# Normalising tokens on VectorE, storing token blocks later, and loading the first pairs' rows in another sequence

## The chip, the core and the metric

The kernel runs on one core of a Trainium2 chip. The metric is the time of one execution on the device, in microseconds. The core has a matrix engine (TensorE, "PE" in the profile), three engines for element-wise work (VectorE, "DVE"; ScalarE, "ACT"; GpSimd, "POOL"), and an engine that does little but issue transfers (SyncE, "SP"). Each engine takes its instructions in the order in which the program was written for it; an instruction that must wait for another engine or for a transfer holds up those behind it on its own engine.

## What is computed

`x` is 2048 tokens of 512 numbers, fp32.

```python
def _A_ref(x, wqkv, wo):                 # 32 heads of 16, no mask
    qkv = (x @ wqkv) -> q, k, v per head
    p = softmax(q k^T * Dh**-0.5)
    return (p @ v, heads side by side) @ wo

def _B_ref(x, w1, w3, w2):               # F = 1792
    h = silu(x @ w1) * (x @ w3)
    return h @ w2

xn = layernorm(x)                        # (x - mean) / sqrt(var + 1e-5)
s = _A_ref(xn, wqkv, wo)
g = silu(_B_ref(xn, w1, w3, w2))
return x + s * g
```

## The kernel before

**Arithmetic.** A product of two fp32 matrices whose precision matters is done as three matmuls: each side is split into a high part and a low part (`xth` and `xtl`, `wh` and `wl`), and high x high, high x low and low x high are added up in one bank of the accumulator memory. So whatever is to be multiplied has first to be split: one engine copies the rounded high part, another subtracts it from the original.

**Two parts.** A prologue (lines 446 to 657) normalises and transposes the tokens, makes the value rows of all heads and the key and query rows of the first four pairs of heads, and finds the score maxima of the first half pair. It takes about 112 of the 1727 us. The main part then runs, for 16 pairs of heads, the scores, the exponentials and the products with the values, and between them the SwiGLU layer and the key and query rows of later pairs. There the order of TensorE's instructions is written out by hand as a string (`ORDER_OF_ISSUE`), and a small model of costs in the program decides only when the helpers of other engines are issued. In the prologue the order on every engine is simply the order of the Python statements.

**The prologue's path for a token tile** (`t`, 128 tokens; four tiles make a block `b` of 512). `load_x` brings `x` to `xin`. `spread` makes mean and variance on VectorE (`st` L492, `mv` L494, `ve` = variance + eps L496) and `rs` = `ve` to the power -1/2 on POOL (L498). `norm` makes `xn` = (`xin` - mean) * `rs` (L505), for the first two tiles on VectorE and for the others on POOL. `transposed` transposes it in four pieces on TensorE (L514), copies the high part on ACT (`xth`, or `xeh` for even blocks, L517) and subtracts on VectorE (`xtl`, `xel`, L518). The two halves of a block are `xts[b]`; `xt` is the pair of tiles that holds blocks 1 and 3.

**Per block.** `token_rows(b, 1)` makes the block's key rows and `token_rows(b, 0)` its query rows (`sh` and `sl`, high and low, for four pairs of heads at once), and stores them to DRAM (`qk`: `sh` by a transfer that ACT issues, L609; `sl` by one that SP issues, L610). `token_values(b, i)` makes the value rows of tile `i`, and ACT issues their store (`v<-vrow`, L547). `beside(b, n)` does score products (L419) of the first pair, four to six at a time, each followed by a maximum on VectorE (L421).

**Loads back from DRAM.** Key and query rows come back with the pairs' heads on other partitions: `load_k(p, cols)` (L398) and `load_q(p, half, cols)` (L407) issue six transfers each on SP. For pair 0, `ks` is loaded block by block as the blocks are made; `load_k(1)` loads all 2048 columns of pair 1. `load_v(1)` (L390) loads the values of the second group of heads into `vt`, at the end of the prologue. `max_rows` turns the maxima into rows `mh` and `ml`, which four small transfers put into `qs` (L446); the first exponential's score product (L675) reads them.

**Weights.** `Weights` streams the units of the SwiGLU weights and of the later projections: `load` (L325) brings a unit to `wr`, `pump` splits it on POOL (L339, L340), `start` issues the first three loads, `fill` issues more as buffers come free.

**Copies of the token blocks.** `xts` of all blocks do not fit in the core's memory, so each block is copied to DRAM (`xt_d`, L624, two transfers of 1 MB) at the top of the block loop. The main part (`gate`) begins with block 3, which is still in place, and fetches blocks 0, 1 and 2 back in pieces later, and block 3 once more for the last projections.

**Completion semaphores.** Each transfer that SP or ACT issues takes one of eight completion semaphores, in turn over both engines, and its issue waits until the transfer that held that semaphore before has landed. In the built program these are the names DMAHW0 to DMAHW7. So adding or moving a transfer changes which earlier one each later one has to wait for.

Of the kernel before, what the change touches and what calls it, by code (L numbers as in the profile page):

```python
# [12 lines left out]
ALU = mybir.AluOpType  # L13
# [8 lines left out]
KC = D // P  # L22
NT = S // P
TB = 4
# [122 lines left out]
def raw(ap):  # L147
    return ap.bitcast(F32)
# [3 lines left out]
def kernel(ctx: ExitStack, tc: tile.TileContext, x, wqkv, wo, w1, w3, w2, out):  # L152
    nc = tc.nc
# [30 lines left out]
    xt_d = [[dram.tile([P, KC * 512], F32R, name=f"xt{b}{s}") for s in range(2)] for b in range(TB)]  # L184
# [23 lines left out]
    def run(gen):  # L208
        for _ in gen:
            pass  # L210
# [105 lines left out]
    class Weights:  # L316
# [37 lines left out]
        def next(self):  # L354

            i = self.taken
            self.taken += 1
            self.pump()
            return i, self.parts.pop(i)
# [4 lines left out]
    wts = Weights()  # L364

    def room_between(n, hf):

        return {0: (0, 2, 5, FH), 1: ()}[hf] if n < KC - 1 else ()
# [23 lines left out]
    def load_k(p, cols=slice(0, S)):  # L392
        t = ks[p % 2]
        for h in range(2):
            r = (p % 4) * 32 + h * DH
            kh, kl = (raw(v)[r:r + DH, cols] for v in qk_d[4 + p // 4])
            for n, src in enumerate((kh, kl, kh)):
                nc.sync.dma_start(raw(t)[64 * h + n * DH:64 * h + (n + 1) * DH, cols], src)  # L398

    def load_q(p, half, c=None):  # L400
        t = qs[p % 2]
        c = c or slice(half * 1024, (half + 1) * 1024)
        for h in range(2):
            r = (p % 4) * 32 + h * DH
            qh, ql = (raw(v)[r:r + DH, c] for v in qk_d[p // 4])
            for n, src in enumerate((qh, qh, ql)):
                nc.sync.dma_start(raw(t)[64 * h + n * DH:64 * h + (n + 1) * DH, c], src)  # L407
# [41 lines left out]
    with tc.tile_pool(name="pro", bufs=1) as pro, tc.tile_pool(name="pros", bufs=1) as pros:  # L449
        wv = [[pro.tile([P, D], F32R, name=f"wv{v}{k}") for v in "hl"] for k in range(KC)]  # L450
        wqk = [[pro.tile([P, KC, P], F32R, name=f"w{c}{v}") for v in "hl"] for c in "qk"]
        xin = [pro.tile([P, D], F32, tag="xin", name=f"xin{t}", bufs=9) for t in range(4)]

        def load_x(t):
            if t >= 4:
                xin.append(pro.tile([P, D], F32, tag="xin", name=f"xin{t}", bufs=9))
            nc.sync.dma_start(xin[t], x[t * P:(t + 1) * P, :])
# [29 lines left out]
        xts = {}  # L487

        def spread(t):

            st = pro.tile([P, 6], F32, tag="st", name="st", bufs=3)
            nc.vector.bn_stats(st, xin[t])  # L492
            mv = pro.tile([P, 2], F32, tag="mv", name="mv", bufs=3)
            nc.vector.bn_aggr(mv, st)  # L494
            ve = pro.tile([P, 1], F32, tag="ve", name="ve", bufs=3)
            nc.vector.tensor_scalar_add(ve, mv[:, 1:2], EPS)  # L496
            rs = pro.tile([P, 1], F32, tag="rs", name="rs", bufs=3)
            nc.gpsimd.tensor_tensor(rs, ve, minus, op=ALU.pow)  # L498
            return mv, rs

        def norm(t, mv=None, rs=None):
            if mv is None:
                mv, rs = spread(t)
            xn = pro.tile([P, D], F32, tag="xn", name="xn", bufs=5)
            (nc.vector if t < 2 else nc.gpsimd).tensor_scalar(xn, xin[t], mv[:, 0:1], rs, op0=ALU.subtract, op1=ALU.mult)  # L505
            return xn

        def transposed(t, xn):
            b, tt = divmod(t, 4)
            if tt == 0:  # L510
                xts[b] = xt_pair(keep) if b % 2 else even_pair()
            ps = bank("m")
            for k in range(KC):
                nc.tensor.transpose(ps[:, k * P:(k + 1) * P], xn[:, k * P:(k + 1) * P], ident)  # L514
            hi, lo = (v[:, :, tt * P:(tt + 1) * P] for v in xts[b])
            src = ps.rearrange("p (k t) -> p k t", k=KC)
            nc.scalar.copy(hi, src)  # L517
            nc.vector.tensor_sub(lo, src, raw(hi))  # L518
# [32 lines left out]
        xn = {0: norm(0)}  # L551
# [35 lines left out]
        def beside(b, n):  # L587

            for _ in range(groups.get((b, n), 0)):
                max_unit(*next(early))  # L590
            if (b, n) == (TB - 1, 4):
                next(first_rows)
                next(first_rows)
# [3 lines left out]
        def token_rows(b, c):  # L597

            hi, lo = xts[b]
            rbk = KC * c  # L600
            ps = bank("e")
            for k in range(KC):
                run(split3(ps, [w[:, k, :] for w in wqk[c]], (hi[:, k, :], lo[:, k, :]), k == 0, k == KC - 1))
            sh = pros.tile([P, 512], F32R, tag="sh", name="sh", bufs=3)
            sl = pros.tile([P, 512], F32R, tag="sl", name="sl", bufs=3)
            nc.scalar.copy(sh, ps)
            nc.vector.tensor_sub(sl, ps, raw(sh))
            cols = slice(b * 512, (b + 1) * 512)
            nc.scalar.dma_start(raw(qk_d[rbk][0])[:, cols], raw(sh))  # L609
            nc.sync.dma_start(raw(qk_d[rbk][1])[:, cols], raw(sl))  # L610

        def more_tokens(n):

            if n < NT:
                transposed(n, xn.pop(n))
                if n + 4 < NT:
                    load_x(n + 4)
                if n + 2 < NT:
                    xn[n + 2] = norm(n + 2)

        for b in range(TB):
            cols = slice(b * 512, (b + 1) * 512)
            for s in range(2):
                nc.sync.dma_start(raw(xt_d[b][s]), raw(xts[b][s]).rearrange("p k t -> p (k t)"))  # L624
            token_rows(b, 1)
            if b == TB - 1:
                load_k(0, cols)
                wts.start()
            beside(b, 0)
            more_tokens(4 * b + 4)  # L630
            if b == 0:
                nc.gpsimd.memset(*next(blank))
                nc.gpsimd.memset(*next(blank))
                more_tokens(5)
            token_rows(b, 0)
            if b < TB - 1:
                load_k(0, cols)
            else:
                load_k(1)
            beside(b, 1)  # L640
            more_tokens(4 * b + (5 if b else 6))
            if b == 0:
                nc.gpsimd.memset(*next(blank))
                nc.gpsimd.memset(*next(blank))
                more_tokens(7)
                load_q(0, 0, cols)
                continue
            for i in range(TB):
                run(token_values(b, i))
                if i == 0 and b < TB // 2:  # L650
                    load_q(0, 0, cols)
                if i == 0 and b == TB - 1:
                    load_q(0, 1)
                    wts.pump(KC)
                    wts.fill()
                if i == 1 and b == 2:
                    load_q(1, 0)
                beside(b, 2 + i)
                if i < 2:
                    more_tokens(4 * b + 6 + i)  # L660
# [99 lines left out]
    def gate():  # L760

        xt = xts[TB - 1]
# [3 lines left out]
        def fetch_tokens(b):  # L766
            pieces.extend((b, s, k) for s in range(2) for k in range(KC))

        def some_tokens():
            for b, s, k in [pieces.pop(0) for _ in range(min(2, len(pieces)))]:  # L770
                nc.sync.dma_start(raw(rows2[s])[:, k, :], raw(xt_d[b][s])[:, k * 512:(k + 1) * 512])
# [21 lines left out]
        for n, b in enumerate(ORDER):  # L793
# [4 lines left out]
            for hf in range(HF):  # L798
# [49 lines left out]
                def counted():  # L848

                    if since[0] is not None:  # L850
                        since[0] += 1
                        if since[0] == 2:
                            since[0] = None
                            fetch_tokens(rest[0])
                    some_tokens()

                for f in range(FH):
                    if f in room_between(n, hf):
                        for e in rows_here():
                            yield e  # L860
                            number += 1
                    for up in range(2):
                        counted()
                        i, w = wts.next()
                        mms = [m for k in range(KC) for m in three([v[:, k, :] for v in w], [v[:, k, :] for v in xt])]
                        yield lambda j, mms=mms: mms[j], 3 * KC, [i], (lambda ps, i, f=f: upped(ps, i, f)) if up else gated, None
                        if up:
                            ups.append(number)
                        number += 1
# [28 lines left out]
                for t in range(4):  # L898
# [10 lines left out]
                    if t > 1 and hf == 1 and n + 1 < TB:  # L909
                        if t == 2:  # L910
                            xt = xt_pair(keep)
                        nc.sync.dma_start(raw(xt[t - 2]).rearrange("p k t -> p (k t)"), raw(xt_d[ORDER[n + 1]][t - 2]))
                    yield down, 3 * FH, [i for i, _ in ws] if t == 3 else [], (
                        lambda ps, i, t=t: summed(ps, i, t)), ups
# [316 lines left out]
    for g in range(KC - 1):  # L1231
        p = 4 * g + 3
# [204 lines left out]
    for t in range(4):  # L1437
        i, ps = take("o")
# [30 lines left out]
```

## Time and profile before

| | |
|---|---|
| median of 3 runs (lowest, highest) | 1729.66 us (1729.29, 1730.66) |
| the profiled execution's own time | 1728.91 us |
| its span in the profile | 1727.1 us |
| mean granted TensorE clock | 0.994 |
| TensorE busy | 1702.8 us, 99% of the span |
| VectorE busy | 1375.0 us, 80% |
| ACT busy | 1221.4 us, 71% |
| POOL busy | 882.8 us, 51% |

All later rows come from that one execution. A row such as `28.45 0.15 DVE L496 TENSOR_SCALAR ve<-mv 128x1 ...` is a line of the timeline: start and duration in microseconds, engine, line of the program, operation, output from input, and in square brackets how long the engine stood still before it and what ended that. "SPq" and "ACTq" are issues of transfers by SP and ACT, so the duration is that of the issue and not of the transfer. A row that starts with two times and a colon is a stretch of the span: its length, then busy time (and number of instructions) of the engines in the order PE, PEld (weight load), DVE, ACT and POOL, then the granted TensorE clock (1.00 is full speed), and at the end the busy share of the transfer engines and the GB/s they moved.

### The profile page before, as it was taken

How to read it: one execution, taken by the hardware profiler on the slowest of the kernel's cores; microseconds unless marked ns; L12 is line 12 of the kernel's file. 1: busy time of each engine (PE TensorE's matmuls, PEld its weight loads, DVE VectorE, ACT ScalarE, POOL GpSimd, SP SyncE). 2: the span in 40 equal slices, each digit the busy share in tenths (PEclk: the TensorE clock that was granted, in tenths of full speed). 3: DMA queues.
4: the chain of work that ended last, by engine and by line, in shares of the span. 5: the costliest groups of instructions: out<-in, count | busy, mean ns of one | idle time of the engine just before them, and what ended most of it. 6: DMA issues, size and time to landing. Idle time of an engine off the chain costs nothing.

```text
span 1727.1 us, 35869 instructions
## 1 busy us (share of the span) xinstructions
PE 1702.8 (99%) x13476; PEld 1133.3 (66%) x13476; DVE 1375.0 (80%) x2299; ACT 1221.4 (71%) x2434; POOL 882.8 (51%) x901
## 2 busy tenths in 40 slices
PE   7989999999999999999999999999999999999998
PEld 6666666666666676666766666667676667665465
DVE  4778888888887887888887887878797878889735
ACT  3217777687777777777777877778777777778861
POOL 8436464276545664466556563556457716652201
PEclk8999999999999999999999999999999999999999
DMA  6773342332345352231435442231333222340732
GB/s 215 250 210 120 117 121 76 51 105 63 84 120 128 114 142 75 64 93 47 106 110 140 130 111 82 78 82 54 99 93 84 79 37 56 99 99 29 219 115 98
DMA packets 170028, 181.07 MB, mean 105 GB/s; under 512 B 43776, under 2 KB 115456, under 8 KB 166624
## 3 DMA queue, kind: packets, MB, share of 16 engines
q1 hardware_dynamic: 165536, 170.66, 36.5%
q10 hardware_dynamic: 4320, 8.13, 1.3%
q8 instruction: 106, 1.74, 0.4%
q14 instruction: 66, 0.54, 0.1%
HBM read 131.56 MB, written 46.11 MB: 103 GB/s over the span
## 4 chain that ended last, share of the span: by engine, by line
PE 88%; issue 6%; POOL 2%; DMA 1%; DVE 1%; SPq 0%; ACT 0%; ACTq 0%; POOLq 0%
PE f L976 31%; PE pv L691 25%; PE m L419 16%; PE e L675 14%; PE m L541 1%; POOL xn L505 1%; DVE mp L421 1%; DMA ovh<-o 0%; PE m L434 0%; POOL rs L498 0%; PE e L201 0%; DMA wl<-o 0%; PE e L203 0%; PE e L205 0%; DMA wr<-in_A_wqkv_dram 0%
## 5 line engine op out<-in xcount | busy, mean ns | idle before, releaser
L421 DVE TENSOR_REDUCE mp<-m 128x1 f32<-128x512 f32 x2048 | 1276.3, 682 | 219.4 <-PE m L419 135.3
L678 ACT ACTIVATE pt<-e 128x512 f32<-128x512 f32 x2048 | 1061.2, 614 | 281.3 <-PE e L675 162.7
L419 PE MATMUL m<-ks,qs 62*128 62x512 f32 x2048 | 743.5, 413 | 7.1 <-DMA qs<-qk 5.2
L675 PE MATMUL e<-qs,ks 64*128 64x512 f32 x2048 | 739.2, 406 | 1.3 <-DMA qs<-ml 1.3
L691 PE MATMUL pv<-pt,vt 128*17 128x512 f32 x4096 | 479.1, 594 | 0.0
L419 PEld LDWEIGHTS m<-ks,qs 62*128 62x128 f32 x2048 | 349.9, 185 | 128.1 <-issue 46.0
L675 PEld LDWEIGHTS e<-qs,ks 64*128 64x128 f32 x2048 | 351.9, 184 | 97.6 <-issue 28.6
L691 PEld LDWEIGHTS pv<-pt,vt 128*17 128x17 f32 x4096 | 100.4, 97 | 250.0 <-issue 244.7
L976 PE MATMUL f<-xtl,wh 64*128 64x512 f32 x496 | 182.5, 391 | 0.0
L976 PE MATMUL f<-xth,wl 64*128 64x512 f32 x496 | 177.8, 393 | 0.0
L976 PE MATMUL f<-xth,wh 64*128 64x512 f32 x496 | 176.2, 392 | 0.0
L976 PE MATMUL f<-wh,hs 64*128 64x512 f32 x528 | 166.0, 392 | 0.0
L976 PE MATMUL f<-xtl,xeh 64*128 64x512 f32 x448 | 164.3, 393 | 0.0
L976 PE MATMUL f<-xth,xeh 64*128 64x512 f32 x448 | 161.7, 394 | 0.0
L828 POOL TENSOR_TENSOR h<-g,h 128x512 f32<-128x512 f32 x56 | 72.0, 1286 | 175.0 <-ACT h L824 171.2
L976 PE MATMUL f<-xth,xel 64*128 64x512 f32 x448 | 160.4, 395 | 0.0
L340 POOL TENSOR_TENSOR wl<-wr,wh 128x512 fp32r<-128x512 f32 x105 | 135.3, 1289 | 8.8
L976 PE MATMUL f<-xeh,hs 64*128 64x512 f32 x368 | 118.7, 394 | 0.0
L340 POOL TENSOR_TENSOR xel<-wr,xeh 128x512 fp32r<-128x512 f32 x87 | 112.1, 1288 | 7.3
L339 POOL TENSOR_SCALAR xeh<-wr 128x512 fp32r<-128x512 f32 x87 | 53.8, 618 | 104.2 <-PE f L976 53.4
L976 PE MATMUL f<-wl,hs 64*128 64x512 f32 x264 | 97.6, 392 | 0.0
L339 POOL TENSOR_SCALAR wh<-wr 128x512 fp32r<-128x512 f32 x105 | 64.9, 618 | 61.3 <-PE f L976 40.8
(213 smaller groups left out, 2161.5 us busy)
## 6 DMA issues: line engine op xcount, KB each, us to landing
wr<-in_B_w_dram SPq DMA_DIRECT2D x168, 256.0 KB
qs<-qk SPq DMA_DIRECT2D x186, 64.0 KB
ks<-qk SPq DMA_DIRECT2D x90, 128.0 KB
ovh<-xt SPq DMA_DIRECT2D x36, 256.0 KB
ovl<-xt SPq DMA_DIRECT2D x36, 256.0 KB
wr<-in_A_wqkv_dram SPq DMA_DIRECT2D x30, 256.0 KB
qk<-ch SPq DMA_DIRECT2D x24, 256.0 KB
qk<-c SPq DMA_DIRECT2D x24, 256.0 KB
```

The costliest lines, as they stand in the source:

```text
L339: nc.gpsimd.tensor_scalar(hi, t, 1.0, 1.0, op0=ALU.mult, op1=ALU.mult)
L340: nc.gpsimd.tensor_sub(lo, t, raw(hi))
L419: nc.tensor.matmul(ps, qs[p % 2][64 * h:64 * h + KM, q0:q0 + P], ks[p % 2][64 * h:64 * h + KM, c * 512:(c + 1) * 512], start=True, stop=True)
L421: nc.vector.reduce_max(mp[p, half][:, h, qt, c:c + 1], ps, axis=AX.X)
L505: (nc.vector if t < 2 else nc.gpsimd).tensor_scalar(xn, xin[t], mv[:, 0:1], rs, op0=ALU.subtract, op1=ALU.mult)
L541: nc.tensor.matmul(ps, lhs, wv[k][h == 1], start=n == 0, stop=n == len(three) - 1)
L675: nc.tensor.matmul(ps, ks[p % 2][64 * h:64 * h + KR, k * P:(k + 1) * P], qs[p % 2][64 * h:64 * h + KR, q0:q0 + 512], start=True, stop=True)
L678: done = nc.scalar.activation(pt, ps, AF.Exp, scale=DH ** -0.5)
L691: nc.tensor.matmul(pv[32 * j:32 * j + VW, :], vt[2 * p // GH][:, key, 2 * p % GH + j % 2, :], pt, start=key < 2 if last else k == 0, stop= ...
L828: nc.gpsimd.tensor_mul(h2, g, h2)
L976: nc.tensor.matmul(ps, left[r], right[r], start=starts and lane == 0, stop=ends and lane == 1)
```

## The change

Three things, all in the prologue but for the last of the copies.

- All sixteen `xn` are made on VectorE. `rs` stays on POOL.
- The copies of the token blocks move. Block 0 is still copied at the top of its loop. Blocks 1 and 2 are copied after their first `token_values` and the `load_q` that stands there. Block 3 is copied in eight pieces of 128 x 512 in the main part, one at each of the first eight products with `w1` or `w3` in the second half of the hidden units of the first block that `gate` does.
- In the last block, `load_q(0, 1)` is issued ahead of `load_k(1)`, where it stood after the first `token_values`. The first three weight loads (`wts.start()`) are issued at the end of block 2, where they stood in block 3 after `load_k(0, cols)`.

```diff
-            (nc.vector if t < 2 else nc.gpsimd).tensor_scalar(xn, xin[t], mv[:, 0:1], rs, op0=ALU.subtract, op1=ALU.mult)
+            nc.vector.tensor_scalar(xn, xin[t], mv[:, 0:1], rs, op0=ALU.subtract, op1=ALU.mult)
...
+        def keep_tokens(b):
+            for s in range(2):
+                nc.sync.dma_start(raw(xt_d[b][s]), raw(xts[b][s]).rearrange("p k t -> p (k t)"))
+
...
         for b in range(TB):
             cols = slice(b * 512, (b + 1) * 512)
-            for s in range(2):
-                nc.sync.dma_start(raw(xt_d[b][s]), raw(xts[b][s]).rearrange("p k t -> p (k t)"))
+            if b == 0:
+                keep_tokens(b)
             token_rows(b, 1)
             if b == TB - 1:
                 load_k(0, cols)
-                wts.start()
             beside(b, 0)
...
             if b < TB - 1:
                 load_k(0, cols)
             else:
+                load_q(0, 1)
                 load_k(1)
...
                 run(token_values(b, i))
                 if i == 0 and b < TB // 2:
                     load_q(0, 0, cols)
+                if i == 0 and 0 < b < TB - 1:
+                    keep_tokens(b)
+                if i == TB - 1 and b == TB - 2:
+                    wts.start()
                 if i == 0 and b == TB - 1:
-                    load_q(0, 1)
                     wts.pump(KC)
                     wts.fill()
...
+        own = [(s, k) for s in range(2) for k in range(KC)]
+
+        def own_tokens():
+            if own:
+                s, k = own.pop(0)
+                nc.sync.dma_start(raw(xt_d[TB - 1][s])[:, k * 512:(k + 1) * 512], raw(xt[s])[:, k, :])
...
                     for up in range(2):
                         counted()
+                        if hf == 1:
+                            own_tokens()
                         i, w = wts.next()
```

The order of TensorE's and of ACT's instructions stays what it was. VectorE gains fourteen instructions. Here is the difference on VectorE around tokens 6 to 8 (the rows of `ve` are each followed by a wait for POOL's `rs` once `xn` stands behind them; `sl` is the low part of the key rows):

```order
 L494 BN_AGGR mv<-st 128x2
 L496 TENSOR_SCALAR ve<-mv 128x1
+L505 TENSOR_SCALAR xn<-xin_353,mv,rs 128x512
 L518 TENSOR_TENSOR xtl<-m,xth 128x4x128
 L492 BN_STATS st<-xin_381 128x6
 L494 BN_AGGR mv<-st 128x2
 L496 TENSOR_SCALAR ve<-mv 128x1
+L505 TENSOR_SCALAR xn<-xin_381,mv,rs 128x512
 L607 TENSOR_TENSOR sl<-e,sh 128x512
 L518 TENSOR_TENSOR xtl<-m,xth 128x4x128
```

Each `xn` now stands between the statistics of its own tile and the work on an earlier tile (`xtl`, `sl`) that followed directly before.

On POOL the same stretch, after the change, holds only `rs`, two weight splits and the four MEMSETs (of `rb`, of `ks` of pair 1 and of both `qs`) that the first block issues:

```order
L525 TENSOR_TENSOR wql<-wr,wqh 128x512
L498 TENSOR_TENSOR rs<-ve,minus 128x1 x3
L635 MEMSET rb 128x512
L636 MEMSET ks_135 128x2048
L498 TENSOR_TENSOR rs<-ve,minus 128x1 x2
L647 MEMSET qs_132 128x2048
L648 MEMSET qs_133 128x2048
L498 TENSOR_TENSOR rs<-ve,minus 128x1 x7
```

Before, an `xn` stood behind each of these `rs` from tile 2 on; the places of `rs` and of the MEMSETs to one another are unchanged.

SP's queue around the loads of the first pairs' rows in the last block, before the change (`qk_75<-sl` is the store of the query rows' low part, `ks_135` are the key rows of pair 1, `qs_132` the query rows of pair 0, `wr` a weight unit; the names after "waits" are completion semaphores and engines):

```order
L610 DMA qk_75<-sl 128x512 [waits DMAHW7_49,DVE_49]
L398 DMA ks_135<-qk_82 16x2048 [waits DMAHW0_49]
...
L398 DMA ks_135<-qk_82 16x2048 [waits DMAHW0_49]
L407 DMA qs_132<-qk_74 16x1024 [waits DMAHW1_49]
L407 DMA qs_132<-qk_74 16x1024 [waits DMAHW2_49]
...
L407 DMA qs_132<-qk_75 16x1024 [waits DMAHW6_49]
L325 DMA wr<-in_B_w_dram 128x4x128 [waits DMAHW7_49]
L390 DMA vt<-v 128x16x68 [waits DMAHW0_49]
L325 DMA wr<-in_B_w_dram 128x4x128 [waits DMAHW1_49,Pool_49]
```

and after it:

```order
L398 DMA ks_134<-qk_83 16x512 [waits DMAHW3_49]
L398 DMA ks_134<-qk_82 16x512 [waits DMAHW4_49]
L610 DMA qk_75<-sl 128x512 [waits DVE_49]
L407 DMA qs_132<-qk_74 16x1024 [waits DMAHW6_49]
L407 DMA qs_132<-qk_74 16x1024 [waits DMAHW7_49]
L407 DMA qs_132<-qk_75 16x1024 [waits DMAHW5_49,DMAHW0_49]
...
L398 DMA ks_135<-qk_82 16x2048
L398 DMA ks_135<-qk_83 16x2048 [waits DMAHW7_49]
...
L325 DMA wr<-in_B_w_dram 128x4x128 [waits DMAHW5_49]
L390 DMA vt<-v 128x16x68 [waits DMAHW6_49,DMAHW0_49]
L325 DMA wr<-in_B_w_dram 128x4x128 [waits DMAHW7_49,Pool_49]
```

The six loads of `qs_132` moved ahead of those of `ks_135`, and with them and the moved copies nearly every transfer of this stretch waits for the landing of another one than before. Of SP's transfers there are six more in all (eight pieces for two whole copies).

## The prediction

> **What bounds the kernel now.** I read the page's totals first, then TensorE's waits before and after 140 us, then windows of the start.
>
> ```profile
> span 1727.1 us, 35869 instructions
> PE 1702.8 (99%) x13476; PEld 1133.3 (66%) x13476; DVE 1375.0 (80%) x2299; ACT 1221.4 (71%) x2434; POOL 882.8 (51%) x901
> PE m L514 <- POOL xn L505: 7.8, 5, 3.8
> PE m L419 <- DMA qs<-qk: 5.2, 1, 5.2
> PE m L419 <- DMA ks<-qk: 1.4, 2, 1.0
> PE e L675 <- DMA qs<-ml: 1.3, 1, 1.3
> ```
>
> TensorE is busy for 99% of the span. The four lower rows are its waits from 0 to 140 us (microseconds in total, times, longest). From 140 to 1700 us the same view lists none, and the order of TensorE's instructions is the same in both kernels. So the change can act only before 140 us, and what TensorE gains or loses there reaches the end one for one. The most that could be gained is these 15.7 us of waits, and what TensorE's clock loses behind them:
>
> ```profile
> 115.00:116.00 1.00, 0.00 (x0) 0.00 (x0) 0.00 (x0) 0.00 (x0) 0.00 (x0) 1.00 0.26 74
> 116.00:117.00 1.00, 0.00 (x0) 0.00 (x0) 0.00 (x0) 0.00 (x0) 0.00 (x0) 0.65 0.29 84
> 122.00:123.00 1.00, 1.00 (x3) 0.34 (x2) 1.00 (x3) 0.00 (x0) 0.00 (x0) 0.50 1.22 295
> 123.00:124.00 1.00, 1.00 (x8) 0.68 (x9) 1.00 (x4) 0.26 (x1) 0.27 (x1) 0.93 1.30 295
> ```
>
> The third number from the right is the granted clock. In the 5.2 us wait it falls to 0.50 about 4 us in, and it is back only at 123.1, 5.5 us after work began again: 5.5 us at half speed lose 2.75 us.
>
> **The normalisation, tokens 2 to 8.** Fourteen `xn` leave POOL for VectorE; `rs` stays on POOL.
>
> ```profile
> 5.45 0.55 DVE L505 TENSOR_SCALAR xn<-xin,mv,rs 128x512 f32<-128x512 f32 x1 [0.76 <-POOL rs L498]
> 8.48 2.71 POOL L525 TENSOR_TENSOR wvl<-wr,wvh 128x512 fp32r<-128x512 f32 x2
> 8.55 1.50 DVE L505 TENSOR_SCALAR xn<-xin,mv,rs 128x512 f32<-128x512 f32 x1
> 28.45 0.15 DVE L496 TENSOR_SCALAR ve<-mv 128x1 f32<-128x1 f32 x1
> 28.52 0.68 DVE L518 TENSOR_TENSOR xtl<-m,xth 128x512 fp32r<-128x512 f32 x1
> 29.12 0.68 DVE L492 BATCH_NORM_STATS2 st<-xin 128x6 f32<-128x512 f32 x1
> 28.69 0.56 POOL L498 TENSOR_TENSOR rs<-ve,minus 128x1 f32<-128x1 f32 x1 [3.95 <-DVE ve L496]
> 29.35 2.08 POOL L505 TENSOR_SCALAR xn<-xin,mv,rs 128x512 f32<-128x512 f32 x1
> 31.48 1.11 PE L514 MATMUL m<-ident,xn 128*128 128x128 f32 x4 [2.66 <-POOL xn L505]
> 31.84 1.80 POOL L633 MEMSET ks<- 128x2048 f32 x1
> 36.40 1.11 PE L514 MATMUL m<-ident,xn 128*128 128x128 f32 x4 [3.81 <-POOL xn L505]
> 38.92 0.80 PE L203 MATMUL e<-xtl,wkh 128*128 128x512 f32 x1
> ```
>
> One `xn` is 2.08 us on POOL and 0.55 on VectorE, but 1.50 beside a POOL instruction that began 0.07 us earlier. VectorE also takes its work in order, and now stands still from `ve` to `rs`: 28.45 + 0.15 + 0.09 + 0.56 + 0.04 makes 0.84 us from the start of `ve`, where the next instruction followed 0.07 us after it. So each norm adds 0.77 + 0.47 = 1.24 us to VectorE (0.47 is 0.55 less its overlap with the next; in the same way an `xtl` takes 0.60 of VectorE's time, 28.52 to 29.12).
>
> Tokens 2 and 3: `xn` stops being late, TensorE gains its two waits there, 1.1 us. Token 6: `rs` comes 1.1 us earlier, and `xn` then ends at about 29.1 instead of 31.43. Token 7's `rs` still stands behind the two MEMSETs on POOL, so it ends at 31.45 and `xn` at 32.05 instead of 36.35. That removes 4.3 us of TensorE's wait, but something else is late next: the K-row product at 38.92 needs `xtl` of token 7, which on VectorE now stands behind `sl`, token 6's `xtl`, and the whole norm of token 8, 32.05 + 0.6 + 0.6 + 1.2 + 0.65: `rs` of token 8 at 35.05. There POOL at once starts the MEMSET of `qs`, as large as that of `ks` (1.80). If that holds VectorE as the row at 8.55 shows, `xn` ends at 37.2 and `xtl` at 37.85; if not, at 35.55 and 36.2. I take the first, the only row of such an overlap: the product starts at 37.9, a gain of **1.0 us** (2.6 by the other end). TensorE is at half clock here before and after.
>
> The Trainium skill (SBUF — State Buffer, "Who interferes with whom") says that VectorE in its two-port mode and a GpSimd instruction exclude each other for a whole instruction, which would hold for a MEMSET too; by it the gain is the 1.0, without it 2.6. No run here shows it for a MEMSET.
>
> **The normalisation, tokens 10 to 15.**
>
> ```profile
> 44.60:85.30 40.70, 38.47 (x182) 27.44 (x180) 32.58 (x62) 11.16 (x23) 16.50 (x13) 1.00 0.73 252
> 47.09 0.37 SPq L624 DMA_DIRECT2D xt<-xth  x1
> 55.49 0.33 SPq L457 DMA_DIRECT2D xin<-in_A_x_dram  x1
> 58.58 0.69 DVE L492 BATCH_NORM_STATS2 st<-xin 128x6 f32<-128x512 f32 x1 [2.48 <-DMA xin<-in_A_x_dram]
> 63.21 0.70 DVE L492 BATCH_NORM_STATS2 st<-xin 128x6 f32<-128x512 f32 x1 [2.87 <-DMA xin<-in_A_x_dram]
> ```
>
> In this stretch VectorE works 32.6 of 40.7 us, so 8.1 are free. Six norms add 6 x 1.24 = 7.4. Of the free time 5.35 us are two waits for x, and these the moved copies should end: before, two 1 MB copies (47.09) go out ahead of the x load at 55.49; now they stand after the loads of `qs`, and the x load is issued at about 45. About 1.2 us of the free time cannot be filled (waits for ACT's copies). So the stretch takes 32.6 + 7.4 + 1.2 = 41.2, **0.5 us longer**, and becomes bound by VectorE: TensorE loses its 1.4 us wait for `ks` but waits for banks instead. From 82.9 us on it runs 1.0 - 0.5 = 0.5 us early.
>
> **The loads.** Each of SP's and ACT's transfers takes one of eight completion semaphores and waits until its last holder has landed.
>
> ```profile
> 97.16 0.36 ACTq L609 DMA_DIRECT2D qk<-sh  x1
> 99.48 0.95 SPq L325 DMA_DIRECT2D wr<-in_A_wqkv_dram  x2
> 100.07 0.73 PE L419 MATMUL m<-ks,qs 62*128 62x512 f32 x4
> 108.94 6.70 SPq L407 DMA_DIRECT2D qs<-qk  x6
> 113.22 0.33 ACTq L547 DMA_DIRECT2D v<-vrow  x1
> 115.34 0.30 SPq L407 DMA_DIRECT2D qs<-qk  x1
> 117.56 0.76 PE L419 MATMUL m<-ks,qs 62*128 62x512 f32 x1 [5.18 <-DMA qs<-qk]
> 116.15 0.51 SPq L390 DMA_DIRECT2D vt<-v  x1
> 118.36 5.47 DVE L421 TENSOR_REDUCE mp<-m 128x1 f32<-128x512 f32 x9 [5.89 <-PE m L419]
> 123.73 0.62 POOL L339 TENSOR_SCALAR wh<-wr 128x512 fp32r<-128x512 f32 x1 [2.81 <-DMA wr<-in_B_w_dram]
> 125.75 0.38 SPq L325 DMA_DIRECT2D wr<-in_B_w_dram  x1
> 126.23 0.80 SPq L446 DMA_DIRECT2D qs<-mh  x1
> 130.37 0.47 PE L675 MATMUL e<-qs,ks 64*128 64x512 f32 x1 [1.27 <-DMA qs<-ml]
> ```
>
> Before, the last `qs` load shares its semaphore with the V store issued at 113.22, so it goes out at 115.3. Now the `qs` loads stand ahead of `ks` of pair 1 and share with nothing later than the V store of token 12: they land some 6 us before use, and the 5.18 us wait goes.
>
> Against that, the fifth load of `ks` for the last block now shares with the Q-row store of 97.16. It lands at 99.45 (before, the `wr` load at 99.48 waited for it). So the last two loads go out at 99.5 and 99.95 and land 2.05 later (the last `qs` load went out at 115.34 and was there at 117.4). TensorE needs them at 100.3: **1.7 us** late. With the 0.5 in hand the prologue ends 1.2 us late, at 113.5 instead of 112.3.
>
> From there TensorE runs at once and at full clock. But the first exponential needs `mh` and `ml` in `qs`, whose loads (126.23) stand on SP behind a weight load (125.75) that waits for POOL's split of unit 4 (123.73 to 125.7), whose load stands behind `vt`, which waits for the V store of token 15. That store moves with the prologue, and from its landing at 115.3 to 126.23 it took 10.9 us; now `vt` is ahead of every weight load but one already landed, which saves 1.8 (0.9 earlier issue, 0.9 for 256 KB less in front at the windows' 290 GB/s). The first exponential comes at 130.37 + 1.2 - 1.8 = 129.8. TensorE gets there at 112.85 + 17 maxima x 0.6 = 123 (VectorE frees its banks, nine of them in 5.47) + 1.2 = 124.1: it stands for 5.7 us. As in the wait of 5.18 the clock falls, now behind this point, where before it was back: **2.75 us** lost. Together 0.6 early and 2.75 lost.
>
> The Trainium skill (TensorE: Matmul & The Clock Gate, "What's actually happening") has the clock halve after an idle window of about 3.4 us and return after as long of work: by it the new wait loses 1.7 us. The trace's 5.5 us is longer, and I keep 2.75.
>
> The eight pieces of the last block's copy go out among the first 36 units of the main part, which has no TensorE wait; its DMAs are the two transfers it had. Their cover is TensorE's 99%; without it each issue is some 0.4 us of SP. I take 0.
>
> **Sum.** -1.0 + 0.5 + 1.7 - 1.8 + 2.75 = +2.1 us on the profiled execution's 1728.9 us (span 1727.1 and 1.8 around it), 1731.0; the runs' median is 0.75 above that execution, so **1731.8 us**. Own range, from MEMSET not blocking (1730.2) and half the clock loss (1728.8) to 2 us more of waits for loads: 1728.8 to 1733.8.
>
> **Rivals.**
> A, the gains pass through. No blocking by the MEMSET (-1.6), the last `ks` loads in time (-1.7), the wait before the exponential short enough to keep the clock (-2.75): 1731.8 - 6.0 = 1725.8. For it: 13 us of waits lose their named cause, and in the wait of 1.27 us at 130.37 the clock held. Against: the three need each other only in part, but each has a row against it.
> B, VectorE becomes the bound, and it is slower. If the x loads are not earlier, the 5.35 us of waits remain and the six norms do not fit: 1731.8 + 5.3 = 1737.1. It decides from the point where x of token 12 lands after about 55 us. For it: VectorE is then at 100%; against: nothing large stands ahead of that load any more.
> C, the change does less than it says: POOL's 2.08 us were hidden except in five places, so only the 1.1 us of tokens 2 and 3 moves, and the `qs` wait merely moves to the exponential at no clock loss: 1728.6.
>
> **How the numbers follow.** Forecast 0.48, A 0.28, B 0.15, C 0.09. This kernel's measurement tells 0.2%, 3.5 us, from no change. Faster takes A and 0.02 of C; same takes most of the forecast and of C, 0.46; slower takes B and 0.09 of the forecast, 0.24. The range 1725.5 to 1735.0 reaches to A and leaves out B.
>
> **What would show it.** Right: no `L514 <- xn` over 3 us; VectorE near 40 us busy or waiting for `rs` from 43 to 84; a wait of 1 to 2 us for `ks` near 100; no wait for `qs<-qk`; 5 to 6 us of wait for `qs<-ml` and a clock of 0.50 behind it. Wrong: the exponential's wait under 3 us, or the clock at 1.00 through it (then A); waits for `xin` as long as before (B); TensorE waits after 140 us.

## The result and the profile after

The changed kernel takes **1734.41 us** (median of 8, 1732.77 to 1738.14), the kernel before 1729.97 (8 runs, 1729.21 to 1732.28): a ratio of 1.0027, 95% interval 1.0016 to 1.0038. So it is 4.4 us slower, where 2.1 were forecast. The profiled execution took 1733.92 us and goes by its span, 5.0 us over that of before.

The totals of the page, and TensorE's waits from 0 to 140 us and after 140 us:

```profile
span 1732.1 us, 35859 instructions
PE 1704.7 (98%) x13476; PEld 1132.9 (65%) x13476; DVE 1389.7 (80%) x2313; ACT 1221.6 (71%) x2434; POOL 854.2 (49%) x887
```

```profile
PE e L682 <- DMA qs<-ml: 5.2, 1, 5.2
PE m L514 <- DVE xn L505: 4.7, 2, 3.0
PE e L203 <- DVE xtl L518: 4.7, 1, 4.7
...
PE m L419 <- DMA ks<-qk: 1.2, 1, 1.2
...
PE m L419 <- DMA ks<-qk: 0.8, 1, 0.8
```

The 5.2 us wait for `qs<-qk` is gone; one of the same length for `ml` has come. The 7.8 us of waiting for `xn` became 4.7 us for `xn` and 4.7 us for `xtl`. The last row lies after 140 us, where the kernel before had no such row.

Since TensorE's order is the same in both kernels, the same instruction can be looked up in both timelines. First before, then after:

```profile
89.84 0.50 PE L201 MATMUL e<-xth,wkl 128*128 128x512 f32 x1
100.73 0.50 PE L541 MATMUL m<-wvh,xtl 128*128 128x512 f32 x1
171.59 0.28 PE L434 MATMUL m<-ident,nm 128*16 128x128 f32 x1
901.09 0.28 PE L434 MATMUL m<-ident,nm 128*16 128x128 f32 x1
949.02 0.28 PE L434 MATMUL m<-ident,nm 128*16 128x128 f32 x1
```

```profile
40.77 0.80 PE L203 MATMUL e<-xtl,wkh 128*128 128x512 f32 x1 [4.68 <-DVE xtl L518]
92.69 0.50 PE L201 MATMUL e<-xth,wkl 128*128 128x512 f32 x1
105.35 0.50 PE L541 MATMUL m<-wvh,xtl 128*128 128x512 f32 x1
132.96 0.76 PE L682 MATMUL e<-qs,ks 64*128 64x512 f32 x1 [5.21 <-DMA qs<-ml]
175.44 0.28 PE L434 MATMUL m<-ident,nm 128*16 128x128 f32 x1
904.98 0.28 PE L434 MATMUL m<-ident,nm 128*16 128x128 f32 x1
954.10 0.28 PE L434 MATMUL m<-ident,nm 128*16 128x128 f32 x1
```

Each row less the row before it gives the size of one term (the K-row product was at 38.92 and the first exponential's product at 130.37 before):

| stretch | late by its end | this stretch | forecast |
|---|---|---|---|
| to the K-row product (tokens 2 to 8) | +1.85 | +1.85 | -1.0 |
| to the key rows of block 3 (tokens 10 to 15) | +2.85 | +1.0 | +0.5 |
| to the value product of token 13 (last `ks` loads) | +4.62 | +1.77 | +1.7 |
| to the first exponential | +2.59 | -2.03 | -1.8 |
| to the second half pair's maxima (clock) | +3.85 | +1.26 | +2.75 |
| to 905 us | +3.89 | 0 | 0 |
| 905 to 954 us | +5.08 | +1.2 | 0 |

Up to the first exponential only one term was badly off. Behind it the clock cost half of what was forecast, and a place in the main part cost about as much as that saved.

### The profile page after: what moved, and what is told of

Its sections match the earlier page's. It is cut to its first block, busy times and chain, and to the rows that moved or that the text cites. A ratio compares the mean times of both kernels' runs of the same rounds, so it can differ in the third digit from the quotient of the medians.

```text
span 1732.1 us, 35859 instructions
## 1 busy us (share of the span) xinstructions
PE 1704.7 (98%) x13476; PEld 1132.9 (65%) x13476; DVE 1389.7 (80%) x2313; ACT 1221.6 (71%) x2434; POOL 854.2 (49%) x887
## 4 chain that ended last, share of the span: by engine, by line
PE 89%; issue 5%; DVE 3%; DMA 1%; SPq 1%; ACT 0%; POOL 0%; ACTq 0%; POOLq 0%
PE f L992 31%; PE pv L698 25%; PE m L419 15%; PE e L682 14%; PE m L541 2%; DVE mp L421 1%; DVE xn L505 1%; DMA ks<-qk 0%; PE e L203 0%; PE e L201 0%; PE m L434 0%; DMA ovl<-o 0%; PE e L205 0%; PE m L514 0%; DMA wr<-in_A_wqkv_dram 0%
## 5 line engine op out<-in xcount | busy, mean ns | idle before, releaser
L339 POOL TENSOR_SCALAR xeh<-wr 128x512 fp32r<-128x512 f32 x87 | 53.9, 619 | 105.0 <-PE f L992 33.8
```

The costliest lines, as they stand in the source:

```text
L339: nc.gpsimd.tensor_scalar(hi, t, 1.0, 1.0, op0=ALU.mult, op1=ALU.mult)
```

## Experiments

Twelve kernels ran, each beside the kernel before. Medians of 5 to 12 executions, and ratios to the kernel before (1730.3 to 1730.4 us beside them):

| run | what it is | us | ratio, 95% interval |
|---|---|---|---|
| u_norm | changed kernel, `xn` on POOL again | 1732.39 | 1.0010 (1.0002 to 1.0019) |
| u_copies | changed kernel, copies where they were | 1734.99 | 1.0025 (1.0015 to 1.0035) |
| u_loads | changed kernel, loads in the old sequence | 1735.73 | 1.0030 (1.0020 to 1.0040) |
| norm_only | kernel before, all `xn` on VectorE | 1739.18 | 1.0048 (1.0034 to 1.0062) |
| m_memset | changed kernel, MEMSETs away from `xn` | 1729.29 | 0.9995 (0.9986 to 1.0004) |
| u_start | changed kernel, `wts.start()` where it was | 1733.71 | 1.0020 (1.0011 to 1.0029) |
| act_rows | changed kernel, first `mh`, `ml` sent by ACT | 1738.60 | 1.0045 (1.0033 to 1.0058) |
| best1 | m_memset and act_rows | 1730.81 | 1.0003 (0.9994 to 1.0012) |
| v_late | changed kernel, `load_v(1)` behind `mh`, `ml` | 1729.80 | 0.9992 (0.9983 to 1.0001) |
| hide_rs | changed kernel, statistics written earlier | 1731.82 | 1.0006 (0.9996 to 1.0015) |
| best3 | m_memset, v_late and hide_rs | 1720.36 | 0.9939 (0.9925 to 0.9952) |
| best3_pool | best3 with `xn` on POOL | 1724.05 | 0.9963 (0.9949 to 0.9977) |

### One part undone, one part alone

```diff
# u_norm, from the changed kernel
-            nc.vector.tensor_scalar(xn, xin[t], ...)
+            (nc.vector if t < 2 else nc.gpsimd).tensor_scalar(xn, xin[t], ...)
# u_copies: keep_tokens(b) for every b at the top of the block loop, no own_tokens()
# u_loads: load_q(0, 1) and wts.start() at their old places
# norm_only, from the kernel before
-            (nc.vector if t < 2 else nc.gpsimd).tensor_scalar(xn, xin[t], ...)
+            nc.vector.tensor_scalar(xn, xin[t], ...)
```

> The change without its first part: tokens 2 to 15 are normalised on POOL again; the moved copies and the new sequence of loads stay. Theory (the traces of before and after, term by term): the prologue runs as before up to the last block's key rows, so the 1.85 us lost at token 7's xtl and the 1.0 us up to the key rows of block 3 go. Three of the last six ks loads still stand behind the query-row store, so about 2 us of wait for ks stay; the first exponential still waits about 5 us for ml, and the clock falls there, about 2.4 us. So some 2 us under the changed kernel: 1732.0 to 1733.0. Rival (all of the loss comes from the normalisation): 1729 to 1730. Rival (the normalisation costs nothing, the loss is from the loads alone): 1734.4.

> The change without its second part: all copies of token blocks at the top of the block loop, as before; all norms on VectorE and the new sequence of loads stay. Theory: the x loads again stand behind two 1 MB copies, VectorE waits for x of tokens 12 and 13 about 2.5 us each and has no free time to make it up, so the prologue comes 2 to 5 us later than in the changed kernel: 1736 to 1739. Rival (the copies are hidden either way): 1734.4 within 1 us.

> The change without its third part: load_q(0,1) and wts.start() where they were; norms on VectorE and moved copies stay. Theory: the wait for ks near 104 us goes (1.8 us), the 5.2 us wait for qs after the last value product comes back and takes the place of the wait for ml, the clock falls once as before. What is left is the delay up to the key rows of block 3, 2.85 us: 1732.5 to 1733.0. Rival (the new sequence of loads is a gain that the norms hide): 1736 to 1737. Rival (the loads are the whole loss): 1730.

> The kernel before with the first part of the change alone: all xn on VectorE. Theory (VectorE held by POOL's MEMSETs, and bound from token 10 on, now with the copies ahead of the x loads): K rows of block 1 some 2 to 3 us late, key rows of block 3 some 4 us late, the wait for qs and the chain behind it as before: 1734 to 1736. Rival (normalising on VectorE alone is harmless, the loss needs the moved copies or loads): 1729.5 to 1731.

`u_norm` came out as the theory had it: the normalisation is 2 us of the changed kernel's loss, the moved transfers the other 2. In its timeline the key rows of block 3 come 2.8 us earlier than in the kernel before (87.04 for 89.84), so the moved transfers do gain inside the prologue; waits for `ks` and `ml`, the clock behind the latter and a wait for `ks` at 934 us (1.5 us) take back more than that.

`u_copies` fell to the rival: with the copies back, VectorE's waits for x are 1.8 us where the kernel before had 5.3, and the time is the changed kernel's within its scatter. So moving the copies is worth next to nothing here by the medians. The profiled executions leave up to 2 us open: the clock of u_copies does not fall at 50.5 us, as the changed kernel's does, and yet it takes 52.3 us from the K-row product to the key rows of block 3, against 51.9.

`u_loads` was 3 us over the theory, nearest to its first rival (1736 to 1737) and 1.3 over the changed kernel, within the scatter of both, and `norm_only` was 3 to 5 over. In both TensorE has a wait that was 0.4 us at most before. Its row and ACT's timeline in norm_only:

```profile
PE m L541 <- ACT vt L548: 2.4, 2, 2.0
```

```profile
108.59 0.59 ACT L546 COPY vrow<-m 128x512 f32<-128x512 f32 x1 [2.54 <-PE m L541]
110.81 0.33 ACTq L547 DMA_DIRECT2D v<-vrow  x1
111.17 0.21 ACT L548 COPY vt<-m 128x64 f32<-128x64 f32 x1 [1.99 <-DMA v<-vrow]
```

ACT stands 1.6 us between the copy of a value row and the issue of its store, and so frees the bank 2 us late. In the built program that store waits for the store of the token before it, which holds the same completion semaphore. The parts do not add up: the normalisation costs 8.8 us alone and 2.0 beside the other two. Of the 8.1 us in norm_only's profiled execution, 4.7 are there by the key rows of block 3, 1.4 more come between the value product of token 13 and the first exponential, where this wait lies, and 1.4 behind it, where the clock is low from 137.0 to 140.4 us. What each part would cost in another combination is not shown.

### What holds VectorE: the MEMSETs

```diff
# m_memset, from the changed kernel (the four MEMSETs of block 0 leave their places)
+        nc.vector.memset(raw(qs[0])[:, 0:1], 0.0)     # behind picks, at 22 us
+        nc.gpsimd.memset(raw(qs[0]), 0.0)
...
+            if b == 2:                                 # behind the xn of token 15
+                nc.vector.memset(raw(qs[1])[:, 0:1], 0.0)
+                nc.gpsimd.memset(raw(qs[1]), 0.0)
+                nc.gpsimd.memset(raw(ks[1]), 1.0)
+                nc.gpsimd.memset(rb, 1.0)
```

> The changed kernel with POOL's four MEMSETs elsewhere: qs of pair 0 at about 22.5 us, after the last xn of block 0's stretch, the others after the xn of token 15 (each behind a one-column MEMSET on VectorE, so that none begins beside an xn). Nothing else is changed. Theory (a MEMSET on POOL holds VectorE's xn until it ends): the two xn of 2.46 and 3.74 us at 28.1 and 36.4 become 0.55 us, the wait of 4.68 us for xtl near 40 goes or falls under 1 us, the prologue comes 3 to 4 us earlier: 1730.0 to 1731.5. Rival (VectorE's order, with xn ahead of xtl, and the wait for rs make xtl late, and the long xn are something else, such as DMA traffic): xn stays long or the wait stays, 1733.5 to 1734.5.

The changed kernel's timeline, VectorE and POOL:

```profile
28.12 2.46 DVE L505 TENSOR_SCALAR xn<-xin,mv,rs 128x512 f32<-128x512 f32 x1 [0.73 <-POOL rs L498]
36.38 3.74 DVE L505 TENSOR_SCALAR xn<-xin,mv,rs 128x512 f32<-128x512 f32 x1 [0.73 <-POOL rs L498]
...
28.03 0.52 POOL L635 MEMSET rb<- 128x512 f32 x1
28.49 1.80 POOL L636 MEMSET ks<- 128x2048 f32 x1
36.29 1.80 POOL L647 MEMSET qs<- 128x2048 f32 x1
38.03 1.80 POOL L648 MEMSET qs<- 128x2048 f32 x1
```

The same two `xn` in m_memset, and then, in the kernel before, the one-column `ve` inside a MEMSET:

```profile
27.76 0.55 DVE L505 TENSOR_SCALAR xn<-xin,mv,rs 128x512 f32<-128x512 f32 x1 [0.73 <-POOL rs L498]
34.12 0.55 DVE L505 TENSOR_SCALAR xn<-xin,mv,rs 128x512 f32<-128x512 f32 x1 [0.73 <-POOL rs L498]
```

```profile
39.78 0.15 DVE L496 TENSOR_SCALAR ve<-mv 128x1 f32<-128x1 f32 x1
...
39.01 1.80 POOL L643 MEMSET qs<- 128x2048 f32 x1
```

An `xn` that begins 0.09 us after a MEMSET ends 0.29 us after the second MEMSET in a row has ended: 36.38 + 3.74 = 40.12 against 38.03 + 1.80 = 39.83. With no MEMSET beside it, it takes 0.55. `ve` keeps its 0.15 us inside a MEMSET, and in m_memset an `xtl` at 79.45 us its 0.68 us inside the MEMSET of 78.94 to 80.75, so not every operation of VectorE is held. The wait for `xtl` falls from 4.7 to 1.7 us, and the time by 5.1 us, 1.5 more than the theory's middle; the kernel is then level with the kernel before. In its timeline the K-row product is 5.4 us earlier (35.32 for 40.77): TensorE stands still 4.0 us less before it, and in front of it the clock is low only from 31.56 us on instead of from 30.03, that is for 3.8 us instead of 10.7.

### The wait for rs

```diff
# hide_rs, in more_tokens(n)
+                of = spread(n + 2) if n + 2 < NT else None
                 transposed(n, xn.pop(n))
...
-                    xn[n + 2] = norm(n + 2)
+                    xn[n + 2] = norm(n + 2, *of)
```

> The changed kernel with the statistics of token n+2 written ahead of the transposition of token n in more_tokens, and its xn behind it. So VectorE does xtl of token n between ve and xn and does not stand still for rs. MEMSETs stay where they are. Theory (each norm costs VectorE 0.77 us of standing still for rs beside its 0.47 us): the prologue from token 10 on, where VectorE has little free time, comes 1 to 2 us earlier, and the MEMSET's hold on xn of token 8 stays: 1732.3 to 1733.5. Rival (only the MEMSETs count, the wait for rs lies beside TensorE's work): 1734 to 1735.

The longest of VectorE's waits from 40 to 92 us, in the changed kernel and in hide_rs:

```profile
DVE xn L505 <- POOL rs L498: 5.8, 8, 0.7
...
```

```profile
DVE sl L607 <- ACT sh L606: 6.8, 3, 5.1
...
```

The eight waits of 0.73 us are gone, and the median falls by 2.6 us, somewhat more than expected. From the K-row product to the key rows of block 3 the timeline takes 49.2 us (39.82 to 89.00) instead of 51.9. Some 0.6 us of that is the clock, which is low for 5.1 us of this stretch instead of 6.3. So from token 10 on VectorE had too little free time to stand still in. Behind it this execution lost most of the gain again, with stretches of low clock from 120.05 and from 130.29 us and waits of 1.2 us at 849 and 937 us; its span is only 0.3 us under the changed kernel's, and the 2.6 us rest on the medians (1728.5 to 1736.2 us here).

### The loads for the last block and the first exponential

```diff
# u_start: wts.start() back behind load_k(0, cols) of block 3; load_q(0, 1) stays first
# act_rows, in max_rows
-                nc.sync.dma_start(raw(qs[p % 2])[r:r + 1, c], raw(v)[8 * h:8 * h + 8, :])
+                (nc.scalar if p == half == 0 else nc.sync).dma_start(raw(qs[p % 2])[r:r + 1, c], raw(v)[8 * h:8 * h + 8, :])
# v_late: load_v(1) leaves the end of the prologue and stands behind these four transfers
+        if p == half == 0:
+            load_v(1)
```

> The changed kernel with wts.start() back in block 3 after load_k(0, cols); load_q(0,1) stays ahead of load_k(1). With it the fifth ks load of the last block no longer shares its completion semaphore with the query-row store; a weight load takes that place. Theory: the wait for ks near 103 to 104 us (1.25 us, and what the last two loads cost in all: 1.8 us) goes, the prologue ends 1.8 us earlier and everything behind it follows: 1732.3 to 1733.0. Rival (the wait for ks has to do with the time of the loads in the transfer engines, not with the semaphore): the wait stays, 1734 to 1735.

> The changed kernel with the four transfers that put mh and ml of the first half pair into qs issued by ACT instead of SP. Nothing else is changed. Theory (the first exponential waits because these transfers stand on SP behind vt and weight loads, not because mh and ml are late): they are issued at about 121 to 124 us, land by 126, and TensorE, which gets there at 127.7, does not wait. The wait of 5.2 us goes and with it the stretch at a clock of 0.50, 1.3 to 1.5 us: 1727.5 to 1728.5. Rival (the transfer engines are full then and the rows are late by any queue): the wait stays above 3 us and the clock still falls, 1732 to 1734.

> The changed kernel with both: POOL's MEMSETs moved away from xn, and the first mh and ml issued by ACT. Theory (the two losses are separate and add): the 5.1 us of the first and about 6.5 us of the second, 1722.5 to 1724. Rival (an earlier prologue only waits longer for weights or the second ks): 1726 or more.

> The changed kernel with load_v(1) moved from the end of the prologue to behind the four transfers of the first mh and ml, all still on SP. It is needed some 170 us later. With it the weight loads of units 4 and 5 no longer stand behind the store of token 15's value rows. Theory (first exponential gated by SP's queue behind vt; in the run that issued the rows by ACT, vt and with it the weight loads slid 5 us later, and POOL's splits, the c store and the copy of g behind them took the 5 us back as a wait of pv): now units 4 and 5 load from about 114 us on, the rows go out at about 123, TensorE does not wait for ml and the clock stays: 1727.5 to 1729. Rival (units 6 and 7 still wait for the same V store, so that the copy of g stands for the store of c and pv waits 3 us or more): 1731 or more.

SP's queue in the changed kernel:

```profile
121.11 0.38 SPq L390 DMA_DIRECT2D vt<-v  x1
...
128.34 0.38 SPq L325 DMA_DIRECT2D wr<-in_B_w_dram  x1
128.82 0.80 SPq L446 DMA_DIRECT2D qs<-mh  x1
```

`u_start` takes the wait for `ks` away (no such row is left before 140 us), so it was the shared semaphore. From the key rows of block 3 to the value product of token 13 it takes 11.2 us instead of 12.7. Its median is only 0.7 us better, less than the 1.8 expected: the wait for `ml` stays at 5.3 us, the clock was low from 129.6 to 136.4 us, where it was low from 132.4 to 135.9 in the changed kernel, and near 851 us TensorE waits 1.1 us for a tile that POOL makes (`hs`), which it does not in the changed kernel.

`act_rows` refuted the simple form of the theory. The wait for `ml` fell to 0.5 us, and the kernel became 4.2 us slower, outside of both theory and rival:

```profile
126.22 0.38 SPq L390 DMA_DIRECT2D vt<-v  x1
145.00 0.59 ACT L822 COPY g<-f 128x512 f32<-128x512 f32 x1 [5.89 <-DMA qk<-ch]
146.14 2.38 PE L698 MATMUL pv<-pt,vt 128*17 128x512 f32 x6 [4.29 <-ACT pt L685]
```

Four transfers of ACT took four of the eight semaphores. In the built program `vt` then waits for the first of them, so it goes out 5 us later, and with it the weight loads. POOL's splits of those weights stand ahead of its split of the projected rows `c`, the store of `c` ahead of ACT's copy `g`, and the exponentials behind `g`: `pv` stands still instead, and the clock is low from 143.9 to 150.8 us. best1 shows the same: 4.6 us of wait for `pt`, and 1730.8 us, where 1722.5 to 1724 were expected of the sum.

`v_late` leaves the rows on SP and takes away what stood ahead of them. Then the chain is shorter without sliding the weights:

```profile
113.81 3.17 SPq L325 DMA_DIRECT2D wr<-in_B_w_dram  x3
...
124.55 0.38 SPq L325 DMA_DIRECT2D wr<-in_B_w_dram  x1
124.97 0.80 SPq L446 DMA_DIRECT2D qs<-mh  x1
...
129.83 0.47 PE L683 MATMUL e<-qs,ks 64*128 64x512 f32 x1 [2.58 <-DMA qs<-ml]
```

The wait is 2.6 us and the clock stays at 1.00 through it. The median is 4.6 us under the changed kernel, a little less than expected, since the wait did not go altogether.

### All three, and the engine once more

best3 is m_memset, hide_rs and v_late together; best3_pool is best3 with the line of `u_norm`.

> The changed kernel with all three: MEMSETs away from xn, the statistics ahead of the transposition, load_v(1) behind the first mh and ml. Theory (separate losses add): 5.1 of the first, 1 to 2 of the second, 6 of the third: 1721 to 1723.5. Rival (an earlier prologue meets the weight chain, POOL's splits of units 4 to 7 behind the V store, so that not all of it passes): 1724 to 1728.

> The kernel with MEMSETs away from xn, statistics ahead of the transposition and load_v(1) behind the first mh and ml, but with xn of tokens 2 to 15 on POOL again, as before. It asks whether VectorE is the right engine once nothing holds it. Theory (on POOL an xn takes 2.08 us and stands behind rs of its own token; TensorE waits for it 8 us in the first 40 us, against 1.7 us with VectorE): the prologue comes 4 to 6 us later than with VectorE, and little of it is given back: 1724 to 1727. Rival (the engine of xn does not matter once the MEMSETs and the load of vt are out of the way): 1720 to 1721.5.

best3's page and its largest waits before 140 us:

```profile
span 1718.3 us, 35857 instructions
...
PE e L203 <- DVE xtl L520: 2.4, 1, 2.4
PE m L516 <- DVE xn L507: 1.7, 2, 1.6
```

The three gains by themselves, 5.1 + 2.6 + 4.6 = 12.3 us, give 1722.1; measured were **1720.36 us**, 10 us under the kernel before and 14 under the changed one. So they are separate losses; the 1.7 us beyond the sum lie within the intervals of the three medians. Between 20 and 140 us the clock is low for 10.2 us in all, where in the changed kernel it is for 20.5. With `xn` on POOL the same kernel takes 1724.05, the better end of its theory, and waits for `xn` and once behind 140 us:

```profile
PE m L516 <- POOL xn L507: 4.8, 4, 2.1
...
PE m L419 <- DMA ks<-qk: 1.0, 1, 1.0
```

So VectorE is the better engine for the normalisation by 3.7 us once nothing holds it. Of the 3.4 us between the two spans 1.4 are lost around this last wait, near 927 us, and not in the prologue. In the kernel as it was changed VectorE was the worse one by 2.

## Why the prediction was right, and where it was not

The time lies within the range and on the side of the forecast, 2.3 us further out by the medians. It is 0.6 us above the narrower range that the prediction worked out from its own terms (1728.8 to 1733.8), and the 4.4 us are more than the 3.5 that the prediction said could be told from no change: it had given 0.24 to a change that can be told as slower, and 0.46 to one that cannot be told. In the profile the sum was +2.1 and came out as +5.0; the first term alone is 2.85 of that difference. The others add nothing, and that is luck: the clock cost 1.5 us less than forecast, and a place in the main part that was put at nothing cost 1.2.

- **What bounds the kernel.** All that matters happens before 140 us: nearly right, though a wait of TensorE after 140 us was named as a sign of being wrong, and one came. 3.85 of the 5.0 us are there by the mark at 175 us, but a `ks` load near 937 us came 0.8 us late, and 1.2 us were lost there. Six of the twelve experiments have such a wait there, of 0.4 to 1.5 us, and the others, like the kernel before, none. In the changed kernel and in v_late SP issues the six loads behind eight stores of `o`, in the kernel before as well. Why the loads come too late in some kernels is not settled.
- **Tokens 2 to 8.** The step that failed: "`xn` ends at 37.2". It counted one MEMSET, where two stood in a row on POOL and VectorE was held through both, and it had `xn` of token 6 end at 29.1, free of any hold, where the MEMSETs of `rb` and `ks` held it to 30.6. So `xn` of token 8 began 1.3 us later than the working has it and ended 2.9 us later, at 40.1. The mechanism, a POOL instruction that holds VectorE, was taken from the right row, and m_memset shows it for a MEMSET; the term was mis-sized, -1.0 for a measured +1.85. By the rule of the Trainium skill (SBUF — State Buffer, "Who interferes with whom") the lock is for a whole instruction; the trace agrees (3.74 us for an `xn` of 0.55), and shows that the waiting one did not get in between two.
- **Tokens 10 to 15.** +1.0 for +0.5. The waits for x went, as forecast, and the copies were their cause: after 40 us the kernels with copies at the top of every block have them (5.3 us before, 1.8 in u_copies, 1.7 in norm_only), the others have none. With `xn` on VectorE they were smaller than the 5.35 us counted on, and u_copies takes the same time. VectorE's standing still for `rs` did count, as hide_rs shows. TensorE also ran at half clock from 50.5 to 53.9 us, which was not forecast; but the half clock at the start of this stretch ended at 43.7 us, 2.9 us into it, and before at 44.6, 5.7 us into it, so that by the clock the two differ by 0.3 us.
- **The loads.** The semaphore shared with the Q-row store: 1.77 for 1.7, and u_start confirms the cause. The chain behind the V store: -2.03 for -1.8. That SP's queue gates the first exponential was right (v_late). What was not seen is that the wait covers a second chain, over POOL's weight splits to the copy `g`, which act_rows laid bare.
- **The clock.** 1.26 for 2.75. The step "The trace's 5.5 us is longer, and I keep 2.75" read one dip as a rule; the 1.7 us that the prediction set beside it was nearer. The next section shows what the dip is.
- **Rivals.** A failed at each of its three conditions: the MEMSET did block, the `ks` loads were late, the wait was long enough for the clock. B's 5.3 us of waits for x did not stay. C is out since TensorE moved by more than it allowed.

## What was not expected of the hardware

The clock moves on a fixed grid. In every one of these traces the stretches at 0.50 last one, two, three or four times 3.41 us, apart from the one that the end of the trace cuts off, and within one trace they begin and end on one grid of that step. Some windows of the grid, of the changed kernel, then of the kernel before, then of best3 (the granted clock is third from the right):

```profile
47.11:50.52 3.41, 2.06 (x10) 0.98 (x8) 2.61 (x7) 0.58 (x1) 0.55 (x1) 1.00 0.43 123
50.52:53.93 3.41, 3.41 (x11) 2.88 (x11) 3.38 (x7) 0.59 (x1) 0.00 (x0) 0.50 0.74 237
129.03:132.44 3.41, 0.00 (x0) 0.00 (x0) 0.66 (x2) 0.00 (x0) 3.33 (x4) 1.00 0.45 140
132.44:135.85 3.41, 2.89 (x14) 2.55 (x16) 0.00 (x0) 1.19 (x2) 3.24 (x4) 0.50 0.84 197
```

```profile
58.29:61.70 3.41, 1.97 (x10) 1.14 (x8) 1.63 (x4) 0.81 (x3) 1.77 (x2) 1.00 0.80 234
61.70:65.11 3.41, 3.41 (x15) 2.38 (x15) 1.76 (x5) 0.00 (x0) 1.43 (x2) 1.00 0.71 209
112.90:116.31 3.41, 0.00 (x0) 0.00 (x0) 0.00 (x0) 0.50 (x2) 0.00 (x0) 1.00 0.51 169
116.31:119.73 3.42, 2.17 (x10) 2.20 (x12) 1.37 (x3) 0.00 (x0) 0.70 (x2) 0.50 0.91 217
```

```profile
92.78:96.19 3.41, 2.27 (x9) 1.15 (x8) 2.10 (x5) 0.80 (x2) 0.00 (x0) 1.00 0.63 182
96.19:99.61 3.42, 3.42 (x9) 2.64 (x8) 1.23 (x3) 0.00 (x0) 0.00 (x0) 0.50 0.35 103
```

In all of these traces an empty window is followed by one at half clock. Whether a second follows went, in these two, with where in its window the wait ended: before, the window after the empty one still had 1.24 us of idle time, and the next, from 119.73 to 123.14, was slow as well; after, the wait ended 0.52 us into the window, and there was no second. It is no threshold: in the kernel before, the slow window from 37.80 has 0.39 us of idle time, and the next is slow too. The wait of 5.2 us cost 1.3 us here, and one of 5.3 us, with two slow windows behind it, cost 1.9 in u_start, by the times of the first exponential's product and of the mark of the second half pair (131.98 and 175.11, against 130.37 and 171.59 before). The Trainium skill (TensorE: Matmul & The Clock Gate, "What's actually happening") states a free-running window of 3413 ns; the traces agree, and the 5.5 us that the prediction kept was one slow window and the rest of another. A window need not be empty, though: 1.35 us without a matmul at 47.11 and 1.14 us in best3 were followed by a slow one, and 1.44 us at 58.29 was not; 0.48 us in hide_rs (from 116.63) was, and 1.80 us in v_late (from 26.07) was not. What decides between these is open.

## What to carry to other kernels

Before an operation moves to another engine, list what both engines will do at that minute, every instruction of a run of them and not the nearest: the gain of moving `xn` was real (3.7 us in best3), but four MEMSETs and a wait for `rs` turned it into a loss of 2. A wait that ends late may hide a second chain of the same length, so take away what stands ahead of it in its queue rather than give it another queue, and look up which completion semaphores the move hands to whom. And price a stall by the clock's windows of 3.41 us, one or two of them at half clock, not by the length of one dip.
